# Transfers moved between queues, a finer second fold level, and a new order of issue in a Fourier and two-layer network kernel

## The chip, the core and the metric

One core of a Trainium2 chip runs the whole program. The metric is the device time of one execution in microseconds (us); lower is better. The engines are PE (matrix products; PEld is its weight load), DVE (vector), ACT (scalar), POOL (GpSimd) and SP (which here only issues transfers). Each takes its own instructions strictly in order and waits on semaphores for the others. ACT, SP and POOL can each issue transfers (DMA); all transfers run on the same 16 DMA engines.

## The reference, cut to what matters

```python
X = np.fft.fft(np.fft.fft(x, axis=1), axis=2).real     # x: (4, 3008, 256)
x = X.reshape(12032, 256)
h = x @ moe_w_in;  r = np.maximum(h, 0);  x = (r * r) @ moe_w_out       # 256 -> 2048 -> 256
h = x @ moe2_w_in; g = h * np.cos(h);     y = g @ moe2_w_out
```

The weights arrive as 64-bit floats. The kernel holds each operand of a product as a high and a low part and makes three products (high by high, low by high, high by low).

## The kernel before, in words

**Transform.** The 3008 points of a sequence are folded by symmetry before they are multiplied with cosine and sine tables. `fold_steps(b, t)` folds group `t` (three groups for each of four sequences `b`) on DVE: `mirrored` (1,024 columns), `eo` twice, `half` twice (512 columns each), `quarter` twice (256 columns each), and for two halves of the result `hi` (a copy on ACT that rounds) and `lo` (the rest, on DVE). For the first sequence the steps up to the first `hi`/`lo` pair (0 to 6) come before the first products and the rest (7 to 10) after; products `T` of part 0 (`cos 0`, `sin 0`) need the first pair, those of part 1 the second. `fold_128` folds one separate column (input `x_mid`, tile `zb`). `finish_first` and `finish` turn the products into the transform's columns: an ACT copy `z`, two DVE sums, a rounding copy on ACT (`xh`, `zh`) and the rest on DVE or POOL (`xl`, `zl`).

**Layer one** runs over 12 column blocks and 16 feature groups, in steps of `mm1` (L527, 6 products), `add` (L534 and L223 on DVE, which reads the products out of PSUM), `act` (three ACT passes, L544 to L547), `lo` (four POOL subtractions on quarters, L557) and, three steps later, `mm2` (L569, 12 products). PSUM holds two `h` tiles, so an `mm1` waits until the `add` two products back is done. **Layer two** does the same over 24 half blocks (L621 and L672).

**Weights.** `conv` turns 64-bit words into a high and a low part with an ACT `Abs` (L166), DVE steps and an ACT copy (L179); it runs between the layer-one steps, and `dft` and `split` fold the transform over the feature axis into the first weight matrix.

**Order.** Every piece of work has a name and a time. `at` collects them, `TIMES` overrides the times of several hundred names, and `issue` sorts by time and emits the work. Within one engine the instructions then run in that order. The times are numbers for sorting, about one unit for each layer-one step (4.1 us).

**Queues before.** All transfers go through SP, except these through POOL: the Fourier matrix (`load_cs`), the tables (`load_tab`, and again for each later sequence by `reload_tab`, since the space holds other data in between), the transform's columns read back (`load_z`, L518), the second weights (`load_w2`, L496) and the second layer's input (`load_o`, L609).

Of the kernel before, what the change touches and what calls it, by code (L numbers as in the profile page):

```python
# [10 lines left out]
F32 = mybir.dt.float32  # L11
# [5 lines left out]
AF = mybir.ActivationFunctionType  # L17
# [4 lines left out]
P = 128  # L22
# [8 lines left out]
NT = 3  # L31
# [5 lines left out]
BLK = 512  # L37
# [7 lines left out]
HALVES = [(2 * c + n * w, w) for c, w in BLOCKS for n in range(2)]  # L45
# [12 lines left out]
TW = (2 * J_A, EES + J_EE + 1)  # L58
# [15 lines left out]
class Order:  # L74
# [5 lines left out]
    def at(self, t, fn, name=None):  # L80
        self.ops.append((TIMES.get(name, t), len(self.ops), fn))

# [6 lines left out]
def f32(ap):  # L89
    return ap.bitcast(F32)  # L90
# [3 lines left out]
def kernel(ctx: ExitStack, tc: tile.TileContext, x, x128, cs, tab0, tab1, w_in1, w_out1, w_in2, w_out2, out):  # L94
    nc = tc.nc
    ctx.enter_context(tc.manual_schedule())
    dram = ctx.enter_context(tc.tile_pool(name="dram", bufs=1, space=DRAM))
# [21 lines left out]
    def buf(tag, name, dt=F32, pool=work, bufs=1, shape=(P, 2, BLK)):  # L119
        return pool.tile(list(shape), dt, name=name, tag=tag, bufs=bufs)  # L120
# [35 lines left out]
    def from_f64(st, hi, lo, sh=None):  # L156
# [36 lines left out]
        def lower():  # L193
            r, unit = (w1.bitcast(F32), 2.0 ** -20) if middle is None else (middle, 2.0 ** -36)
            v.scalar_tensor_tensor(out=lo, in0=r, scalar=unit, in1=got["a"].bitcast(F32), op0=ALU.mult, op1=ALU.mult)

        return [size, guard, mask, merge, rest, power] + [join] * (middle is None) + [lower]


    raws, dat, jobs = {}, {}, {}  # L200
    tabs = [[buf(f"t{i}{t}", f"t{i}{t}", F32R, fft, 1, (P, 2, TW[i])) for t in range(NT)] for i in range(2)]
    cs_sb = []
    u128 = [buf(f"u128{p}", f"u128{p}", F32R, fft, 1, (P, 4, NT, B)) for p in "hl"]

    def load_tab(i, t):
        nc.gpsimd.dma_start(out=tabs[i][t], in_=(tab0, tab1)[i][t])

    def reload_tab(i, t):
        tabs[i][t] = buf(f"t{i}{t}", f"t{i}{t}", F32R, fft, 1, (P, 2, TW[i]))
        load_tab(i, t)  # L210

    def load_cs():
        cs_sb.extend(buf(f"cs{p}", f"cs{p}", F32R, fft, 1, (P, 2, D)) for p in "hl")
        for p, src in zip(cs_sb, cs):
            nc.gpsimd.dma_start(out=p, in_=src.rearrange("(k p) d -> p k d", p=P))

    def load_x(b, t, bufs):
        raws[b, t] = bufs
        for i, r in enumerate(bufs):
            nc.sync.dma_start(out=r, in_=x[b, t, i].rearrange("p a e d -> p (a e d)").rearrange("p (h n) -> p h n", h=2))  # L220

    def tt(out, in0, in1, op):
        nc.vector.tensor_tensor(out=out, in0=in0, in1=in1, op=op)  # L223
# [6 lines left out]
    def fold_steps(b, t):  # L230

        x = {}

        def views():
            ra, rb = raws.pop((b, t))
            x["a"], x["b"] = ra, rb
            x["eo"] = units(rb, "p (e a d) -> p e a d", e=2, a=4)

            x["f"] = units(ra, "p (i a b d) -> p i a b d", i=2, a=2, b=2)
            x["fv"] = units(ra, "p (a b d) -> p a b d", a=4, b=2)  # L240

            x["g"] = units(rb, "p (i a d) -> p i a d", i=4, a=2)

            x["src"] = (units(ra, "p (a n) -> p a n", a=4)[:, 1:3], units(rb, "p (a n) -> p a n", a=4)[:, 0:2])

        def mirrored():
            views()
            tt(x["a"], x["a"], x["b"], ALU.add)

        def eo(i):  # L250
            ab = units(x["a"], "p (a e d) -> p a e d", a=4, e=2)
            tt(x["eo"][:, i], ab[:, :, 0], ab[:, :, 1], PM[i])

        def half(i):
            tt(x["f"][:, i], x["eo"][:, :, 0::2], x["eo"][:, :, 1::2], PM[i])

        def quarter(i):
            tt(x["g"][:, i], x["fv"][:, 0:4:3, 0], x["fv"][:, 0:4:3, 1], PM[i])

        def hi(i):  # L260
            if i == 0:
                x["p"] = [buf(f"d{p}", f"d{p}", F32R, fft, NT, (P, 2, 2, 2 * P)) for p in "hl"]
                dat[b, t] = [p.rearrange("p a b (u d) -> p (a b u) d", d=P) for p in x["p"]]
            nc.scalar.activation(x["p"][0][:, i], x["src"][i], AF.Copy)  # L264

        def lo(i):
            tt(x["p"][1][:, i], x["src"][i], f32(x["p"][0])[:, i], ALU.subtract)

        return [mirrored] + [lambda i=i, fn=fn: fn(i) for fn, i in (
            (eo, 0), (eo, 1), (half, 0), (half, 1), (hi, 0), (lo, 0), (quarter, 0), (quarter, 1), (hi, 1), (lo, 1))]  # L270
# [11 lines left out]
    def load_128():  # L282
        raws["mid"] = scratch(2, NT, 4, B)
        nc.sync.dma_start(out=raws["mid"], in_=x128)
# [114 lines left out]
    def load_w1(c, bufs):  # L399
        for k, st in enumerate(bufs):  # L400
            nc.sync.dma_start(out=st.rearrange("p h n -> p (h n)").rearrange("p (n t) -> p n t", t=2),
                              in_=src_in(w_in1, k, c * FCH * P, FCH * P))
            wi[c, k] = st.rearrange("p h n -> p (h n)").rearrange("p (n t) -> p n t", t=2)
# [89 lines left out]
    def load_w2(name, c):  # L493
        parts = w_chunk("a" if name == "in" else "b")
        for p, src in zip(parts, w2_dram[name, c]):
            nc.gpsimd.dma_start(out=p, in_=src)  # L496
        (wi2 if name == "in" else wo2).append(parts)
# [16 lines left out]
    def load_z(k, i):  # L514
        c, w = BLOCKS[k]
        if i == 0:
            load_zb(k, x_buf())
        nc.gpsimd.dma_start(out=xt[1, k][i][:, :, :w], in_=z_dram[i][:, :, c:c + w].rearrange("i p w -> p i w"))  # L518
# [86 lines left out]
    def load_o(k):  # L605
        c, w = HALVES[k]
        parts = x_buf()
        for p, o in zip(parts, o_dram):
            nc.gpsimd.dma_start(out=p[:, :, :w], in_=o[:, :, c:c + w].rearrange("m p w -> p m w"))  # L609
        xt[2, k] = parts  # L610
# [64 lines left out]
    def l2_out(k):  # L675
        c, w = HALVES[k]
        o = buf("AB"[k % 2] + "0", "o")
        a = accs.pop((2, k))
        nc.scalar.activation(o[:, 0, :w], a[:, 0, :w], AF.Copy)
        nc.vector.tensor_copy(o[:, 1, :w], a[:, 1, :w])  # L680
        for m in range(2):
            nc.sync.dma_start(out=out[m][:, c:c + w], in_=o[:, m, :w])
# [42 lines left out]
    def fold(times, b, t):  # L725
        got = []

        def step(j):
            if j == 0:
                got.extend(fold_steps(b, t))  # L730
            got[j]()

        for j, when in enumerate(times):
            at(when, lambda j=j: step(j), ("fold", b, t, j))
# [15 lines left out]
    for t in range(NT):  # L750
        fold([-80 + t + 0.05 * j for j in range(7)] + [0.02 + 0.1 * t + 0.01 * j for j in range(4)], 0, t)
        for i, job in enumerate(JOBS[::2]):
            at(-79.5 + t + 0.01 * i, lambda t=t, i=i, job=job: start_first(job, ps_a, f"acc{i}", (t,)), ("T", 0, i, t))
        at(-79.45 + t, lambda t=t: job_128(0, (t,)), ("job_128", 0, t))
        at(-78.7 + 0.01 * t, lambda t=t: load_tab(1, t), ("tab", 1, t))
# [21 lines left out]
    for key in KEYS:  # L777
        span = 1.5
        if isinstance(key, tuple):
            c, k = key  # L780
            convert(t, span, key, lambda c=c, k=k: conv_w1(c, k))
            if k:
                end = t + span
                at(end, lambda c=c: dft_w1(c), ("dft", c))
                at(end + 0.1, lambda c=c: split_w1(c), ("split", c))
                at(end + 0.8, lambda c=c: load_wc(c), ("load_wc", c))
                if c < NCH - 1:
                    at(end + 0.01, lambda c=c: load_w1(c + 1, pair("B", I32)), ("load_w1", c + 1))
        else:
            convert(t, span, key, lambda f=key: conv_wo1(f))  # L790
            if key < NF - 4:
                at(t + span, lambda f=key + 4: load_wo1(f, buf(f"A{f // 2 % 2}", "wo", I32)), ("load_wo1", key + 4))
        t += span


    for b, (load, start, gap, t1, gap1) in {1: ((14, 21, 21.6), 26, 4, 38.4, 1.5), 2: ((53, 53.5, 54), 54, 4.6, 68, 2), 3: ((76, 76.5, 77), 78, 4.6, 92, 2)}.items():
        for t in range(NT):
            at(load[t], lambda b=b, t=t: load_x(b, t, staged(t)), ("load_x", b, t))
            fold([start + gap * t + gap / 11 * j for j in range(11)], b, t)
        for i in range(2):  # L800
            for t in range(NT):

                at(start + gap * ((i * NT + t) // 2 + 1) + 0.1, lambda i=i, t=t: reload_tab(i, t), ("tab", b, i, t))
        for i, job in enumerate(JOBS):
            def begin(b=b, job=job):
                jobs[b, job] = ps_h.tile([P, 2, BLK], F32, name="h")
                transform(job, jobs[b, job], lhs_of(b), P)

            at(t1 + gap1 * i + 0.2, begin, ("T", b, *job))
            finish(t1 + gap1 * i + 0.9, b, job, lambda b=b, job=job: jobs[b, job], lambda: pair("B", F32R), 0.3)  # L810
# [175 lines left out]
```

## Time and profile before

| what | value |
|---|---|
| median of 3 runs | 1945.47 us (1945.16 to 1946.25) |
| profiled execution | 1946.22 us, of which 1944.4 us lie between its first and last instruction (the span) |
| PE busy | 1893.9 us, 97% of the span |
| ACT, DVE, POOL busy | 76%, 70%, 59% |
| granted PE clock, mean | 0.993 |

Every "idle" below is idle time of an engine before one instruction, with what ended it. A busy share is an average over stages with different limits, so the stages are looked at one by one.

### The profile page before, as it was taken

The numbers are of one execution on the slowest core, as the hardware profiler recorded it, in microseconds if no ns is written. First come the engines' busy times: TensorE is split into PE (matmuls) and PEld (weight loads), VectorE is DVE, ScalarE is ACT, GpSimd is POOL, SyncE is SP. The second block draws the span as 40 slices with busy tenths as digits, with TensorE's granted clock in tenths as the row PEclk, the third lists the DMA queues.
The fourth block names the chain that finished last, engine by engine and source line by source line (L and its number), as shares of the span: only waits on it lengthen the run. The fifth ranks groups of instructions, "written<-read, shape, count | busy, mean of one in ns | idle before, by whom it ended". The sixth has DMA issues, their size and how long they took to land.

```text
span 1944.4 us, 23842 instructions
## 1 busy us (share of the span) xinstructions
PE 1893.9 (97%) x8544; PEld 1572.1 (81%) x8544; DVE 1361.7 (70%) x1563; ACT 1482.8 (76%) x1537; POOL 1139.8 (59%) x1105
## 2 busy tenths in 40 slices
PE   6799999999999999999999999999999999999999
PEld 4577787777888888888888888888888888888887
DVE  7789858769576776765766666666666666666666
ACT  3788777768788888887877777777777777777776
POOL 1567887768787778786544444444444444444442
PEclk8899999999999999999999999999999999999999
DMA  7544443443443343436111111121111111111110
GB/s 274 171 150 136 145 128 140 151 139 113 150 143 132 123 140 117 141 123 192 55 33 32 32 32 33 33 59 37 33 32 33 33 32 44 51 33 33 32 32 21
DMA packets 76153, 173.22 MB, mean 89 GB/s; under 512 B 9072, under 2 KB 32640, under 8 KB 76036
## 3 DMA queue, kind: packets, MB, share of 16 engines
q1 hardware_dynamic: 50692, 108.32, 16.4%
q0 software_dynamic: 25344, 63.39, 11.2%
q8 instruction: 67, 1.10, 0.2%
q14 instruction: 50, 0.41, 0.1%
HBM read 112.90 MB, written 58.79 MB: 88 GB/s over the span
## 4 chain that ended last, share of the span: by engine, by line
PE 77%; DVE 3%; issue 1%; ACT 1%; DVEq 0%; ACTq 0%
PE acc L672 26%; PE h L621 18%; PE acc L569 16%; PE acc L621 9%; PE h L527 8%; PE h L310 1%; DVE s L223 1%; DVE inT L223 1%; DVE u L534 0%; DVE r L635 0%; ACT s L545 0%; ACT s L544 0%; ACT gh L547 0%; ACT dh L264 0%; DVE ol L223 0%
## 5 line engine op out<-in xcount | busy, mean ns | idle before, releaser
L660 POOL TENSOR_TENSOR gl<-r,gh 128x1024 fp32r<-128x1024 f32 (+2 forms) x189 | 445.0, 2355 | 541.5 <-ACT gh L653 471.7
L557 POOL TENSOR_TENSOR gl<-s,gh 128x256 fp32r<-128x256 f32 (+2 forms) x768 | 593.7, 804 | 206.2 <-ACT gh L547 168.7
L635 DVE SCALAR_TENSOR_TENSOR r<-n,h 128x1024 f32<-128x1024 int32 (+2 forms) x129 | 154.7, 1199 | 219.2 <-ACT n L627 199.7
L544 ACT ACTIVATE s<-s 128x1024 f32<-128x1024 f32 (+2 forms) x192 | 199.6, 1040 | 106.6 <-DVE s L223 103.0
L223 DVE TENSOR_TENSOR s<-u,h 128x512 f32<-128x512 f32 (+2 forms) x384 | 242.7, 673 | 23.3 <-POOL gl L557 1.3
L627 ACT ACTIVATE n<-h 128x1024 int32<-128x1024 f32 (+2 forms) x129 | 130.3, 1010 | 160.9 <-PE h L621 160.8
L569 PE MATMUL acc<-gl,wbh 128*128 128x512 f32 (+2 forms) x768 | 237.4, 389 | 4.5 <-POOL gl L557 4.4
L569 PE MATMUL acc<-gh,wbh 128*128 128x512 f32 (+2 forms) x768 | 238.2, 392 | 2.1 <-DVE ol L223 2.1
L635 DVE SCALAR_TENSOR_TENSOR r<-n,r 128x1024 f32<-128x1024 int32 (+2 forms) x192 | 233.4, 1216 | 6.6
L569 PE MATMUL acc<-gh,wbl 128*128 128x512 f32 (+2 forms) x768 | 235.3, 388 | 0.0
L534 DVE SCALAR_TENSOR_TENSOR u<-zb,wc,h 128x512 f32<-128x512 f32 (+2 forms) x192 | 140.6, 732 | 132.5 <-PE h L527 131.5
L643 ACT ACTIVATE r<-r,halfpi 128x1024 f32<-128x1024 f32 (+2 forms) x192 | 218.4, 1137 | 6.2
L545 ACT ACTIVATE s<-s 128x1024 f32<-128x1024 f32 (+2 forms) x192 | 200.5, 1044 | 6.1
L547 ACT ACTIVATE gh<-s 128x1024 fp32r<-128x1024 f32 (+2 forms) x192 | 200.5, 1044 | 6.1
L672 PE MATMUL acc<-gh,wbh 128*128 128x512 f32 (+2 forms) x768 | 202.8, 386 | 0.0
L672 PE MATMUL acc<-gh,wbl 128*128 128x512 f32 (+2 forms) x768 | 202.8, 386 | 0.0
L672 PE MATMUL acc<-gl,wbh 128*128 128x512 f32 (+2 forms) x768 | 202.8, 386 | 0.0
L621 PE MATMUL h<-xh,wah 128*128 128x512 f32 (+2 forms) x516 | 199.0, 386 | 1.1 <-DVE r L223 1.1
L642 ACT ACTIVATE r<-r 128x1024 f32<-128x1024 f32 (+2 forms) x192 | 198.2, 1032 | 1.9 <-DVE r L635 1.8
L621 PE MATMUL h<-xl,wah 128*128 128x512 f32 (+2 forms) x516 | 198.9, 386 | 0.0
L621 PE MATMUL h<-xh,wal 128*128 128x512 f32 (+2 forms) x516 | 198.9, 386 | 0.0
L653 ACT ACTIVATE gh<-r 128x1024 fp32r<-128x1024 f32 (+2 forms) x192 | 197.1, 1027 | 0.4 <-DVE r L223 0.4
(144 smaller groups left out, 3344.1 us busy)
## 6 DMA issues: line engine op xcount, KB each, us to landing
inT<-x_in SPq DMA_DIRECT2D x18, 512.0 KB, 6.6
t<-tab_in POOLq DMA_DIRECT2D x12, 756.0 KB, 5.9
t<-tab_in POOLq DMA_DIRECT2D x12, 752.0 KB, 5.9
oh<-oh SPq DMA_DIRECT2D x16, 512.0 KB, 2.9
ol<-ol SPq DMA_DIRECT2D x16, 512.0 KB, 4.6
xh<-oh POOLq DMA_DIRECT2D x16, 512.0 KB, 4.2
xl<-ol POOLq DMA_DIRECT2D x16, 512.0 KB, 5.1
y_out<-o SPq DMA_DIRECT2D x32, 256.0 KB, 3.7
```

The lines of the kernel that those rows point to most:

```text
L223: nc.vector.tensor_tensor(out=out, in0=in0, in1=in1, op=op)
L544: nc.scalar.activation(s[:, :, :w], s[:, :, :w], AF.Relu)
L545: nc.scalar.activation(s[:, :, :w], s[:, :, :w], AF.Square)
L547: nc.scalar.activation(hi[:, :, :w], s[:, :, :w], AF.Copy)
L557: nc.gpsimd.tensor_tensor(out=lo[:, n, cols], in0=s[:, n, cols], in1=f32(hi)[:, n, cols], op=ALU.subtract)
L569: nc.tensor.matmul(accs[1, k][m][:, n, :w], wt, g[:, n, :w], start=begin and i == 0, stop=end and i == 2)
L621: nc.tensor.matmul(a[:, j, :w], st, mv[:, m, :w], start=m == 0 and q == 0, stop=m == 1 and q == 2)
L635: nc.vector.scalar_tensor_tensor(out=r[:, :, :w], in0=n[:, :, :w], scalar=-c, in1=src[:, :, :w], op0=ALU.mult, op1=ALU.add)
L642: nc.scalar.activation(r[:, :, :w], r[:, :, :w], AF.Abs)
L643: nc.scalar.activation(r[:, :, :w], r[:, :, :w], AF.Sin, bias=halfpi, scale=-1.0)
L660: e.tensor_tensor(out=lo[:, :, :w], in0=r[:, :, :w], in1=f32(hi)[:, :, :w], op=ALU.subtract)
L672: nc.tensor.matmul(accs[2, k][:, m, :w], w_out_t([c[part] for c in wo2], f, m), g[:, j, :w], start=f == 0 and q == 0, stop=f == NF - 1 and ...
```

## The change

1. **Later transfers by SP.** `reload_tab`, `load_z`, `load_w2` and `load_o` (104 issues) go from POOL's queue to SP's. `reload_tab` reads from copies of the six tables in device memory, which six new transfers (`copy_tab`, device memory to device memory, 752 or 756 KB each) make between steps 9 and 15 of layer one.
2. **First transfers by two engines.** Of each pair of transfers of the first weights and of the first sequence, SP issues one and ACT the other; the middle column is loaded by ACT and first. Later pairs stay on SP.
3. **Half of the second fold level later.** For the first sequence `half` (two steps of 512 columns) becomes four steps `some` of 256 columns; two stand ahead of the first `hi`/`lo` pair, two after it, so a group has 13 steps instead of 11.
4. **Output tiles.** `l2_out` uses one tile for each of the two output halves instead of one for both; the very last output half is issued by ACT.
5. **New order.** `TIMES` is replaced (605 names instead of 540).

```diff
+    tab_dram = {(i, t): dram.tile([P, 2, TW[i]], F32, name=f"tab{i}{t}") for i in range(2) for t in range(NT)}
+
+    def copy_tab(i, t):
+        nc.sync.dma_start(out=tab_dram[i, t], in_=(tab0, tab1)[i][t])
     def reload_tab(i, t):
         tabs[i][t] = buf(f"t{i}{t}", f"t{i}{t}", F32R, fft, 1, (P, 2, TW[i]))
-        load_tab(i, t)
+        nc.sync.dma_start(out=f32(tabs[i][t]), in_=tab_dram[i, t])
+    def queues(n):
+        return (nc.sync, nc.sync if n else nc.scalar)
     def load_x(b, t, bufs):
         raws[b, t] = bufs
-        for i, r in enumerate(bufs):
-            nc.sync.dma_start(out=r, ...)
+        for e, i, r in zip(queues(b), range(2), bufs):
+            e.dma_start(out=r, ...)
...
+        def some(ia):
+            i, a = ia
+            tt(x["f"][:, i, a], x["eo"][:, a, 0::2], x["eo"][:, a, 1::2], PM[i])
+        halves = [(some, (0, 1)), (some, (1, 0))] if b == 0 else [(half, 0), (half, 1)]
+        others = [(some, (0, 0)), (some, (1, 1))] if b == 0 else []
-            (eo, 0), (eo, 1), (half, 0), (half, 1), (hi, 0), (lo, 0), (quarter, 0), ...
+            (eo, 0), (eo, 1), *halves, (hi, 0), (lo, 0), *others, (quarter, 0), ...
...
     def load_128():
-        nc.sync.dma_start(out=raws["mid"], in_=x128)
+        nc.scalar.dma_start(out=raws["mid"], in_=x128)
...
     def load_w1(c, bufs):
-        for k, st in enumerate(bufs):
-            nc.sync.dma_start(...)
+        for e, k, st in zip(queues(c), range(2), bufs):
+            e.dma_start(...)
...
     def load_w2(name, c):
-            nc.gpsimd.dma_start(out=p, in_=src)
+            nc.sync.dma_start(out=f32(p), in_=src)
...
     def load_z(k, i):
-        nc.gpsimd.dma_start(out=xt[1, k][i][:, :, :w], ...)
+        nc.sync.dma_start(out=f32(xt[1, k][i])[:, :, :w], ...)
...
     def load_o(k):
-            nc.gpsimd.dma_start(out=p[:, :, :w], ...)
+            nc.sync.dma_start(out=f32(p)[:, :, :w], ...)
...
     def l2_out(k):
-        o = buf("AB"[k % 2] + "0", "o")
-        nc.scalar.activation(o[:, 0, :w], a[:, 0, :w], AF.Copy)
-        nc.vector.tensor_copy(o[:, 1, :w], a[:, 1, :w])
-        for m in range(2):
-            nc.sync.dma_start(out=out[m][:, c:c + w], in_=o[:, m, :w])
+        os = [buf("AB"[k % 2] + str(m), "o", shape=(P, 2, BLK))[:, 0, :w] for m in range(2)]
+        nc.scalar.activation(os[0], a[:, 0, :w], AF.Copy)
+        nc.vector.tensor_copy(os[1], a[:, 1, :w])
+        for m, e in enumerate((nc.sync, nc.scalar if k == len(HALVES) - 1 else nc.sync)):
+            e.dma_start(out=out[m][:, c:c + w], in_=os[m])
...
+    for n, (i, t) in enumerate((i, t) for i in range(2) for t in range(NT)):
+        at(9.37 + n, lambda i=i, t=t: copy_tab(i, t), ("copy_tab", i, t))
```

What the new `TIMES` does to the order, engine by engine. PE: at the start `T sin 0` of group 0 before `T cos 0`; then a dozen single swaps of neighbouring `mm1` and `mm2`, the first of them `mm1` 5 ahead of `mm2` 2. DVE: `fold_128` moves from behind step 2 of the second weight piece to the very front; `split` 0 moves between the two `some` of group 1; the sums of the middle column (`end_128`) move ahead of those of `cos 0`; the late fold steps of the first sequence are reordered so that group 0 comes last; in layer one about 20 `add` move ahead of one or two `conv` steps, and two `fold` steps of later sequences move forward. ACT: the `xh` copies of `cos 0` move ahead of the `z` copy of `sin 0`; the copy of `part` (0, 1) moves from before `split` 1 to after it; a few single swaps. POOL: two swaps near the start.

## Rows read from the trace of the kernel before

**Rows 1.** Busy time by stretch; columns are named in the first line.
```profile
core 0: us, PE busy (x) PEld busy (x) DVE busy (x) ACT busy (x) POOL busy (x), PEclk, DMA share, GB/s
0.00:60.00 60.00, 35.84 (x186) 24.97 (x186) 44.77 (x82) 24.12 (x41) 15.43 (x26) 0.88 0.69 240
60.00:115.00 55.00, 48.19 (x187) 37.08 (x186) 44.45 (x72) 42.45 (x49) 32.13 (x40) 0.91 0.57 180
...
340.00:372.00 32.00, 28.05 (x112) 21.25 (x111) 30.28 (x34) 24.29 (x27) 22.40 (x30) 0.95 0.47 160
...
sum 1944.40, PE 1893.87 PEld 1572.12 DVE 1361.69 ACT 1482.77 POOL 1139.81; mean PE 270.55 PEld 224.59 DVE 194.53 ACT 211.82 POOL 162.83
```

**Rows 2.** Timeline of PE, 344 to 490 us: start, us, instruction, [idle before <-releaser].
```profile
347.94 0.50 PE L527 MATMUL h<-xh,wah 128*128 128x512 f32 x1 [1.24 <-DVE s L223]
...
361.70 0.50 PE L527 MATMUL h<-xh,wah 128*128 128x512 f32 x1 [0.63 <-DVE s L223]
365.25 0.50 PE L527 MATMUL h<-xh,wah 128*128 128x512 f32 x1 [1.88 <-DVE s L223]
...
432.93 0.49 PE L527 MATMUL h<-xh,wah 128*128 128x480 f32 x1 [1.86 <-DVE s L223]
...
486.05 0.95 PE L310 MATMUL h<-t,dh 128*128 128x376 f32 x4 [1.64 <-DVE s L223]
```

**Rows 3.** Busy time in one stretch after the third of these waits; columns as in Rows 1.
```profile
366.30:369.70 3.40, 3.40 (x9) 2.21 (x8) 3.29 (x5) 3.34 (x4) 1.77 (x3) 0.50 0.88 348
```

**Rows 4.** Timeline of DVE, 340 to 482 us.
```profile
340.70 3.39 DVE L223 TENSOR_TENSOR dl<-inT,dh 128x512 fp32r<-128x512 f32 x1 [1.63 <-ACT dh L264]
...
351.59 2.15 DVE L223 TENSOR_TENSOR inT<-inT 128x512 f32<-128x512 f32 x2
...
422.79 8.01 DVE L223 TENSOR_TENSOR inT<-inT 128x512 f32<-128x512 f32 x2
...
481.30 2.74 DVE L223 TENSOR_TENSOR inT<-inT 128x256 f32<-128x256 f32 x1
```

**Rows 5.** Timeline of POOL around the first two DVE rows of Rows 4.
```profile
339.93 0.74 POOL L518 DMA_DIRECT2D xl<-zl  x1
340.69 2.84 POOL L557 TENSOR_TENSOR gl<-s,gh 128x256 fp32r<-128x256 f32 x4
...
351.31 3.73 POOL L557 TENSOR_TENSOR gl<-s,gh 128x256 fp32r<-128x256 f32 x4 [4.18 <-ACT gh L547]
```

**Rows 6.** Timeline of ACT, DVE and PE, 4 to 43 us.
```profile
4.71 0.66 ACT L166 ACTIVATE f64t<-inA 128x512 f32<-128x512 f32 x1 [2.69 <-DMA inA<-w_in]
...
11.02 0.79 DVE L223 TENSOR_TENSOR zb<-zb 128x48 f32<-128x48 f32 x6
...
12.11 0.21 DVE L223 TENSOR_TENSOR u128l<-zb,u128h 128x48 fp32r<-128x48 f32 x1 [0.31 <-ACT u128h L296]
...
16.43 2.62 DVE L223 TENSOR_TENSOR inB<-inB 128x512 f32<-128x512 f32 x4
...
30.66 0.96 PE L310 MATMUL acc<-t,dh 64*128 64x376 f32 x8 [2.12 <-ACT dh L264]
...
37.20 0.41 DVE L223 TENSOR_TENSOR inB<-inB 128x256 f32<-128x256 f32 x1
37.54 0.41 DVE L223 TENSOR_TENSOR in<-in 128x256 f32<-128x256 f32 x1
...
41.44 1.46 DVE L223 TENSOR_TENSOR dl<-in,dh 128x512 fp32r<-128x512 f32 x2
```

**Rows 7.** Transfers: destination<-source, issuing queue, count, size, median us to landing.
```profile
t<-tab_in POOLq DMA_DIRECT2D x12, 752.0 KB, 5.9
...
inA<-w_in SPq DMA_DIRECT2D x2, 512.0 KB, 4.9
```

**Rows 8.** Timeline of ACT at 91 us: the longest wait for a weight transfer.
```profile
91.30 0.69 ACT L166 ACTIVATE mid<-inB 128x512 f32<-128x512 f32 x1 [2.68 <-DMA inB<-w_in]
```

**Rows 9.** Timeline of DVE at the end of the span.
```profile
1940.62 0.66 DVE L680 COPY o<-acc 128x484 f32<-128x484 f32 x1 [4.26 <-ACT o L679]
```

More of the change, by code (lines that the diff above doesn't have):

```diff
@@ L215, in load_cs @@
             nc.gpsimd.dma_start(out=p, in_=src.rearrange("(k p) d -> p k d", p=P))
+    def queues(n):
+        return (nc.sync, nc.sync if n else nc.scalar)
     def load_x(b, t, bufs):
         raws[b, t] = bufs
-        for i, r in enumerate(bufs):
-            nc.sync.dma_start(out=r, in_=x[b, t, i].rearrange("p a e d -> p (a e d)").rearrange("p (h n) -> p h n", h=2))
+        for e, i, r in zip(queues(b), range(2), bufs):
+            e.dma_start(out=r, in_=x[b, t, i].rearrange("p a e d -> p (a e d)").rearrange("p (h n) -> p h n", h=2))
     def tt(out, in0, in1, op):
@@ L267, in lo @@
             tt(x["p"][1][:, i], x["src"][i], f32(x["p"][0])[:, i], ALU.subtract)
+        def some(ia):
[3 more added lines that the diff above has]
+        others = [(some, (0, 0)), (some, (1, 1))] if b == 0 else []
         return [mirrored] + [lambda i=i, fn=fn: fn(i) for fn, i in (
-            (eo, 0), (eo, 1), (half, 0), (half, 1), (hi, 0), (lo, 0), (quarter, 0), (quarter, 1), (hi, 1), (lo, 1))]
+            (eo, 0), (eo, 1), *halves, (hi, 0), (lo, 0), *others, (quarter, 0), (quarter, 1), (hi, 1), (lo, 1))]
     def scratch(*shape):
@@ L399, in load_w1 @@
     def load_w1(c, bufs):
-        for k, st in enumerate(bufs):
-            nc.sync.dma_start(out=st.rearrange("p h n -> p (h n)").rearrange("p (n t) -> p n t", t=2),
+        for e, k, st in zip(queues(c), range(2), bufs):
+            e.dma_start(out=st.rearrange("p h n -> p (h n)").rearrange("p (n t) -> p n t", t=2),
                               in_=src_in(w_in1, k, c * FCH * P, FCH * P))
@@ L517, in load_z @@
             load_zb(k, x_buf())
-        nc.gpsimd.dma_start(out=xt[1, k][i][:, :, :w], in_=z_dram[i][:, :, c:c + w].rearrange("i p w -> p i w"))
+        nc.sync.dma_start(out=f32(xt[1, k][i])[:, :, :w], in_=z_dram[i][:, :, c:c + w].rearrange("i p w -> p i w"))
     def l1_mm1(k, f):
@@ L608, in load_o @@
         for p, o in zip(parts, o_dram):
-            nc.gpsimd.dma_start(out=p[:, :, :w], in_=o[:, :, c:c + w].rearrange("m p w -> p m w"))
+            nc.sync.dma_start(out=f32(p)[:, :, :w], in_=o[:, :, c:c + w].rearrange("m p w -> p m w"))
         xt[2, k] = parts
@@ L750 @@
     for t in range(NT):
-        fold([-80 + t + 0.05 * j for j in range(7)] + [0.02 + 0.1 * t + 0.01 * j for j in range(4)], 0, t)
+        fold([-80 + t + 0.05 * j for j in range(7)] + [0.02 + 0.1 * t + 0.01 * j for j in range(6)], 0, t)
         for i, job in enumerate(JOBS[::2]):
```

2 lines of the change are left out of this document (1 added, 1 removed).

## The prediction

> **What bounds the kernel now.** I read the busy time by stretch first. PE works for 1893.87 of 1944.40 us [rows 1], so 50.5 us of idle time, and the stretches in which PE's clock is granted at its lower level, are all that this change can win; it takes no product away. The idle time is uneven: 24.2 us lie before 60 us, 6.8 us between 60 and 115, and 4.0 us in the 32 us from 340 on, where DVE is busy for 30.28 of 32 [rows 1]. So I asked PE's own timeline there what it waited for. Five waits between 344 and 490 us, 1.24, 0.63, 1.88, 1.86 and 1.64 us, all end with a DVE sum (`add` releasing an `h` tile) [rows 2]: 7.25 us. After the third, PE runs 3.4 us at half its clock (granted 0.50, the 1.2 GHz level) although it is busy all the time [rows 3]; that costs 1.7 us more.
>
> Then: why is DVE late? Its timeline shows four instructions over 2 us between 340 and 482 us; the first took 3.39 us, the longest pair 8.01 us and the last 2.74 us [rows 4]. A 512-column fold step elsewhere takes 2.62 / 4 = 0.655 us [rows 6], and the 256-column step starts 0.34 us after its like (37.20 to 37.54) [rows 6]. So these cost 2.7, 6.7 and 2.3 us too much. They have two inputs in SBUF, and POOL is at work beside them. POOL's timeline shows what is special: the first begins at 340.70, right behind POOL's transfer instruction (339.93 to 340.67), and lasts until POOL's run of four subtractions is nearly over (340.69 to 343.53) [rows 5]. A fold pair that meets such a run without a transfer ahead of it (POOL from 351.31) takes 2.15 us for two: it is delayed by 0.8 us, and POOL's run stretches to 3.73 instead of 2.84 us, so the two take turns [rows 4, 5]. All four long ones follow a POOL transfer instruction by less than 1 us. I read this as: behind a transfer issued by POOL, DVE is not let in until POOL falls idle. Each long one is followed within 8 us by waits of rows 2: 340.70 by 347.94, the second by 361.70 and 365.25, 422.79 by 432.93, 481.30 by 486.05.
>
> **Part 1, later transfers by SP.** POOL no longer issues them, so the long instructions should become ordinary ones (+0.8 us a pair at most). DVE's `add` then comes 2.3 to 6.7 us earlier, more than each wait of PE, so the whole waits go: -7.25 us. The fall of the clock follows only the closest two of them (0.63 and 1.88 within 4 us); without them I expect no fall: -1.7 us. Bounds: 0 if the long instructions come from something else, -9.0 if all goes. I take -8.9, the sum as it stands, since every one of the four has its POOL transfer.
>
> The Trainium skill states a rule against this reading (SBUF — State Buffer, section "SBUF: two separate sides"): DVE and GpSimd share one port pair as an exclusive lock, which whoever starts first holds for one instruction, whoever issued a transfer before. The 0.8 us for a pair agree with it, the 3.39 us do not. By the rule alone the sum would lose the -8.9 us; that is rival A.
>
> SP's queue takes 104 issues more. It is in order: where a `load_z` waits for a `z` store to land, the next `load_x`, table or store waits behind it. These have some steps of 4 us in hand before they are needed; I take 0, with the upper end under rival C. The six table copies move about 4.5 MB through the same engines while weights are loaded; each load behind one lands later by the copy's own time, at most the 5.9 us that a table took [rows 7]. ACT already waits for such loads, up to 2.68 us [rows 8], without PE standing still there. I take +1.0 us, nearer the lower end, since even the longest of ACT's waits now leaves PE at work; bounds 0 and +5.9.
>
> **Parts 2, 3 and the new order at the start.** PE waits 2.12 us at 30.66 for the fold of group 2 [rows 6]. Until then DVE works almost without a break, so its path counts:
> - `fold_128` leaves it: 0.79 + 0.31 (its wait) + 0.21 = -1.30 us [rows 6]. Its new place is idle time of DVE before the first weight conversion, but its last piece waits for an ACT copy queued behind `Abs`, about 0.45 us after `Abs` ends, and the conversion queues behind it: +0.45.
> - `some` instead of `half`: per group 2 x 0.655 become 2 x 0.34, so 3 x 0.63 = -1.89 us.
> - The first weight piece shares the engines with the second instead of preceding it. ACT now waits for it until 4.71 us [rows 6]; the two landed 4.9 us after issue in the mean [rows 7], the first 0.75 to 4.66, so 3.9, the second then 5.9. If both land together, the first comes up to 2.0 us later; if each queue runs at its own speed, 0. I take +0.4, nearer the lower end, since the transfer starts from empty engines. ACT's own five issues and its table load fill time in which it waits anyway (2.69 us idle) [rows 6].
> - `split` 0 between two `some` makes the rounding copy of group 1 wait for one more ACT copy: +0.3.
>
> Sum -2.04 us, just inside PE's 2.12 us of idle time, so the products of group 2 start that much earlier. Next comes `T cos 1`, which needs the late fold steps; they ended at 42.90 (41.44 + 1.46) [rows 6]. They now hold six `some` more, 6 x 0.34 = +2.04, but `end_128` (about 1.1 us) moves into DVE's idle time and two small waits go (1.1 us), so they end near 42.90 - 2.04 + 2.04 - 2.2 = 40.7. `T cos 1` started during them and now must wait for group 0, the last, and needs 1.75 us more: it ends 1.7 us earlier. All that follows to 60 us hangs on it in the same order. I take -1.7 us; bounds -3.0 (the conversion is not late at all, and a clock fall goes too) and +1.0 (the first piece 2 us late).
>
> The remaining swaps (an `add` ahead of a `conv` step, `part` behind `split`) may move waits of about 1 us between 60 and 200 us either way: 0, bounds -4 and +3.
>
> **Part 4, the end.** DVE's last copy waits for ACT's because both write one tile [rows 9]. Side by side, the last transfer is issued about 0.6 us earlier: -0.6 us; 0 if the wait has another cause. Before that PE covers both copies.
>
> **Sum** against the profiled execution of 1946.22 us (1944.4 of span and 1.8 around it): -8.9 + 1.0 - 1.7 - 0.6 = -10.2, so 1936.0 us. The median of the runs stands 0.75 us lower, so 1935.3 us.
>
> **Rivals.**
> - A. *The long DVE instructions are not the transfers' doing*, only an unlucky meeting with POOL's runs. For it: POOL is as busy after the change. Against it: the run from 351.31 met a fold pair and let it in. Then 1945.5 + 1.0 - 1.7 - 0.6 = 1944.2 us: no change.
> - B. *The order and the lighter queues clear other waits too.* DVE is busy 44.45 of 55 us between 60 and 115 [rows 1]; if half of the 6.8 us of idle time there, and a third of the clock's loss (granted 0.91 over 55 us: 0.09 x 55 = 5 us), go as well, 1935.3 - 3.4 - 1.7 = 1930.2 us. Against it: most steps there stay in their old order.
> - C. *SP's queue becomes the wait.* A `load_x` or a weight load stands behind a copy or a waiting `load_z`, DVE reaches the fold or `conv` step first, and being in order it holds up `add` and so PE. Each costs up to 5.9 us [rows 7], with no slack to cover it where ACT already waits, as at 91 us [rows 8]. Four such are 23.6 us: 1935.3 + 23.6 - 1.0 = 1958 us. It decides from three on (17.7 us); against it, the loads keep their lead of several steps.
>
> **How the numbers follow.** Forecast (faster by 4 to 14 us) 0.64, B 0.15, A 0.13, C 0.05, and 0.03 for a start so late that it eats the rest. No change means within 0.2%, 3.9 us, about what a measurement of this kernel tells from none. Of A, 0.01 falls on either side of it, and of the late start 0.02 within it: faster 0.64 + 0.15 + 0.01 = 0.80; same 0.11 + 0.02 = 0.13; slower 0.05 + 0.01 + 0.01 = 0.07. The range must leave out 2 in 10: below, 1928, under B; above, 1943, the forecast's sum with the copies at their upper end (+4.9) and the start at its (+2.7), just short of A. The forecast's own range is 1931 to 1941.5.
>
> **What would show it.** Right: no DVE instruction over 2 us between 100 and 600 us; no POOL transfer after 10 us; PE idle under 1 us in 340 to 372, at full clock; the products of group 2 at about 28.6 us; `T cos 1` ending 1.7 us earlier; DVE's last copy beside ACT's. Wrong: long DVE instructions beside POOL runs that have no transfer ahead (A); PE waits released by `add` behind a DVE or ACT wait on a transfer (C); ACT's first `Abs` after 6 us.

## The result, and the profile after

The changed kernel takes 1929.27 us (median of 4 runs, 1928.63 to 1930.15) against 1945.86 us for the kernel before on the same chip: ratio 0.9914, 95% interval 0.9897 to 0.9931, so 16.6 us less. The forecast was 1935.3 us with a range of 1928 to 1943. The sign and the range were right; the size was not: the time lies below the forecast's own range (1931 to 1941.5) and near rival B's 1930.2. The profiled execution took 1928.63 us, with a span of 1926.9 us.

Busy time by stretch of the changed kernel; columns as in [rows 1].

```profile
0.00:60.00 60.00, 35.12 (x185) 24.19 (x186) 45.62 (x89) 24.93 (x43) 16.40 (x28) 0.91 0.71 241
60.00:115.00 55.00, 50.18 (x200) 38.59 (x199) 46.96 (x75) 44.00 (x49) 28.29 (x38) 0.94 0.64 211
115.00:340.00 225.00, 221.83 (x1017) 182.25 (x1016) 182.51 (x250) 179.65 (x189) 169.92 (x212) 1.00 0.46 158
340.00:372.00 32.00, 30.39 (x141) 24.53 (x141) 25.25 (x35) 25.75 (x28) 23.39 (x30) 1.00 0.46 168
372.00:500.00 128.00, 128.00 (x642) 108.56 (x641) 87.32 (x124) 97.82 (x104) 95.91 (x125) 1.00 0.38 133
```

Against [rows 1], DVE falls from 30.28 to 25.25 us between 340 and 372 and PE rises from 28.05 to 30.39 at full clock. Before 60 us nothing is won: PE 35.12 against 35.84 us. DVE's timeline of the changed kernel, with the steps that answer to [rows 4]: the `dl` behind the wait for `dh`, two pairs of `half`, and a `quarter`.

```profile
333.99 0.82 DVE L232 TENSOR_TENSOR dl<-inT,dh 128x512 fp32r<-128x512 f32 x1 [1.62 <-ACT dh L273]
...
347.93 2.37 DVE L232 TENSOR_TENSOR inT<-inT 128x512 f32<-128x512 f32 x2
...
413.37 2.02 DVE L232 TENSOR_TENSOR inT<-inT 128x512 f32<-128x512 f32 x2
...
466.61 0.60 DVE L232 TENSOR_TENSOR inT<-inT 128x256 f32<-128x256 f32 x1
```

The four took 3.39, 3.87 (a pair, of which the first step is the prediction's second long instruction; its row of the kernel before is shown next), 8.01 (a pair) and 2.74 us before; now 0.82, 2.37, 2.02 and 0.60.

```profile
355.70 3.87 DVE L223 TENSOR_TENSOR inT<-inT 128x512 f32<-128x512 f32 x2
```

PE's timeline of the changed kernel in the same stretch: of the five waits of [rows 2] none is left after 372 us, and `T cos 0` of the last sequence, which waited 1.64 us at 486.05, starts without a wait at 469.57. Two smaller waits stand between 340 and 372 us:

```profile
355.52 0.50 PE L543 MATMUL h<-xh,wah 128*128 128x512 f32 x1 [0.50 <-DVE s L232]
...
358.29 0.73 PE L585 MATMUL acc<-gh,wbh 128*128 128x512 f32 x2 [1.11 <-DVE ol L232]
...
469.57 0.85 PE L326 MATMUL h<-t,dh 128*128 128x376 f32 x4
```

The start is where the forecast fails. ACT's timeline of the changed kernel:

```profile
0.74 0.41 ACTq L300 DMA_DIRECT2D zb<-x_mid  x1
1.18 0.46 ACTq L417 DMA_DIRECT2D inA<-w_in  x1
1.67 0.45 ACTq L229 DMA_DIRECT2D inB<-x_in  x1
2.15 3.69 ACTq L229 DMA_DIRECT2D in<-x_in  x2
5.87 1.28 ACT L166 ACT_TABLE_LOAD   x1 [5.87 <-DMA zb<-x_mid]
7.16 0.66 ACT L166 ACTIVATE f64t<-inA 128x512 f32<-128x512 f32 x1
```

`Abs` starts at 7.16 us and waits for no piece of the weights: before it stand ACT's five issues and the table load. The row of 3.69 us is two issues with a wait between them. The fourth issue ends at 3.18 us and the fifth begins only at 5.50, as a narrower view shows (ACT, then DVE):

```profile
5.50 0.34 ACTq L229 DMA_DIRECT2D in<-x_in  x1
```

```profile
5.50 0.79 DVE L232 TENSOR_TENSOR zb<-zb 128x48 f32<-128x48 f32 x6 [4.63 <-DMA zb<-x_mid]
```

At 5.50 the middle column has landed, ACT's first transfer. In the trace the fifth issue waits for that transfer's semaphore and uses the same one again. In half_unsplit and the three probes, which keep these issues, it begins at 5.74, 5.64, 5.51 and 5.78 us, each time together with DVE's fold of that column. So 2.32 of the 3.69 us are a wait for a landing and not work of issuing. Before, `Abs` started at 4.71 us [rows 6]. The `dh` product of group 2 starts at 30.16 us against 30.66 [rows 6], not at 28.6, and the late fold steps end at 42.37 (41.68 + 0.69) against 42.90, not at 40.7:

```profile
30.16 0.95 PE L326 MATMUL acc<-t,dh 64*128 64x376 f32 x8
...
41.70 1.12 PE L326 MATMUL acc<-t,dh 128*128 128x188 f32 x4 [0.17 <-ACT dh L273]
```

```profile
41.68 0.69 DVE L232 TENSOR_TENSOR dl<-inB,dh 128x512 fp32r<-128x512 f32 x1
```

And at the end DVE's copy still waits for ACT's (ACT's takes 0.57 us from 1922.31), just as in [rows 9], though each now has its own output tile:

```profile
1922.91 0.66 DVE L696 COPY o<-acc 128x484 f32<-128x484 f32 x1 [4.26 <-ACT o L695]
```

### The profile page after: what moved, and what is told of

Its sections match the earlier page's. It is cut to its first block, busy times and chain, and to the rows that moved or that the text cites. A ratio compares the mean times of both kernels' runs of the same rounds, so it can differ in the third digit from the quotient of the medians.

```text
span 1926.9 us, 23833 instructions
## 1 busy us (share of the span) xinstructions
PE 1887.8 (98%) x8544; PEld 1570.3 (81%) x8544; DVE 1346.0 (70%) x1569; ACT 1481.3 (77%) x1537; POOL 1070.1 (56%) x1001
## 4 chain that ended last, share of the span: by engine, by line
PE 81%; DVE 0%; ACT 0%; issue 0%; DVEq 0%; ACTq 0%
PE acc L688 27%; PE h L637 18%; PE acc L585 18%; PE acc L637 9%; PE h L543 9%; PE h L326 1%; DVE s L232 0%; DVE inT L232 0%; DVE u L550 0%; DVE ol L232 0%; ACT s L560 0%; ACT s L561 0%; ACT gh L563 0%; ACT oh L611 0%; DVE o L696 0%
```

## The experiments

To see where each kernel wins, I compare the start of the same product in PE's timelines: kernel less kernel before, in us, negative is earlier. The columns are named products with their start in the kernel before; the last column compares the spans. Each is one profiled execution.

| kernel | `T sin 1`, 44.42 | `mm1` 14, 117.85 | `mm1` 63, 342.45 | `T cos 0` of sequence 3, 486.05 | span |
|---|---|---|---|---|---|
| changed kernel | +0.06 | -2.70 | -5.37 | -16.48 | -17.5 |
| part1_alone | -0.02 | +0.33 | +1.81 | -9.89 | -9.9 |
| part1_copies_late | +0.02 | +0.49 | -0.62 | -12.35 | -12.3 |
| order_alone | -1.92 | -6.71 | -8.42 | -13.74 | -14.8 |
| part1_undone | +1.82 | -0.94 | -3.53 | -8.82 | -9.9 |
| old_order | +3.31 | +4.56 | +5.98 | -5.77 | -5.7 |
| first_by_sp | -0.14 | -3.16 | -5.11 | -16.28 | -17.4 |
| half_unsplit | -0.19 | -3.47 | -4.95 | -16.54 | -17.6 |
| parts_1_4_5 | -2.07 | -6.25 | -7.02 | -18.57 | -19.5 |
| parts_1_4_5_copies_late | -0.81 | -3.06 | -7.12 | -18.64 | -19.7 |

My theory after the result: part 1 wins what the long DVE instructions cost (342 to 486 us), ACT's issues spoil the start, and something else, order or lighter POOL, wins the 5.4 us between 44 and 342. Rivals: A (the transfers are not the cause), and that order and part 1 win the same waits.

**Part 1 by itself.** The kernel before with (cut to the lines that matter):

```diff
-            nc.gpsimd.dma_start(out=p, in_=src)
+            nc.sync.dma_start(out=f32(p), in_=src)
...
-        nc.gpsimd.dma_start(out=xt[1, k][i][:, :, :w], ...)
+        nc.sync.dma_start(out=f32(xt[1, k][i])[:, :, :w], ...)
...
-            nc.gpsimd.dma_start(out=p[:, :, :w], in_=o[...])
+            nc.sync.dma_start(out=f32(p)[:, :, :w], in_=o[...])
...
-        load_tab(i, t)
+        nc.sync.dma_start(out=f32(tabs[i][t]), in_=tab_dram[i, t])
...
+        at(9.37 + n, lambda i=i, t=t: copy_tab(i, t), ("copy_tab", i, t))
```

> The kernel before with part 1 alone: the 104 later transfers by SP and the six table copies; the old order, start and end. Theory (DVE is shut out behind a transfer that POOL issues): no DVE instruction over 2 us between 100 and 600 us, the five PE waits of 1.24, 0.63, 1.88, 1.86 and 1.64 us gone, the time 9 to 12 us below that of before, 1934 to 1937 us. If SP's lighter partner POOL also explains the 5.4 us that the changed kernel gains between 60 and 340 us, up to 17 us below, 1929 us. Rival A (the long instructions are an unlucky meeting with POOL's runs): within 2 us of before, long instructions still there.

Ratio 0.9946 (0.9934 to 0.9959); the span is 9.9 us shorter. All of it is won between 342 and 486 us, 11.7 us; before that it is 1.81 us behind. No DVE instruction with work over 2 us is left between 100 and 600 us. ACT's and then PE's timeline of this kernel show what it lost:

```profile
122.75 0.66 ACT L166 ACTIVATE mid<-wo 128x512 f32<-128x512 f32 x1 [4.98 <-DMA mid<-w_out]
```

```profile
127.40 0.77 PE L532 MATMUL h<-xh,wah 128*128 128x480 f32 x1 [2.54 <-DVE s L228]
```

**The copies' share**, part 1 alone with:

```diff
-        at(9.37 + n, lambda i=i, t=t: copy_tab(i, t), ("copy_tab", i, t))
+        at(20 + 1.5 * n, lambda i=i, t=t: copy_tab(i, t), ("copy_tab", i, t))
```

> Part 1 alone, its six table copies moved from steps 9 to 15 to steps 20 to 28 of layer one, when the weights of layer one are loaded. In part 1 alone ACT waits 4.98 us at 122.75 for a weight transfer and PE 2.71 us behind it at 127.40, and it is 5.97 us behind the kernel before at 128 us. Theory (the copies delay those loads): ACT's wait under 1 us, PE never over 2 us behind the kernel before, 2 to 4 us below part 1 alone, 1930 to 1933 us in the trace. Rival (the weights are late because SP's queue has more to issue in order): the waits stay, within 1 us of part 1 alone.

Ratio 0.9930 (0.9918 to 0.9943), span 2.4 us shorter than with the early copies. ACT's wait for the same transfer:

```profile
118.42 0.68 ACT L166 ACTIVATE mid<-wo 128x512 f32<-128x512 f32 x1 [0.50 <-DMA mid<-w_out]
```

4.98 us has become 0.50, and the kernel is never more than 2 us behind the kernel before (1.94 us, at 86 us). The two intervals overlap; the trace shows where the 2.4 us come from: the copies delayed the weights, and SP's longer queue did not.

**Part 1 undone** in the changed kernel (the edit above backwards).

> The changed kernel with part 1 undone: the later transfers by POOL again, tables read again from the inputs, no copies; new order, start and end kept. Theory: long DVE instructions come back behind POOL's transfers, 9 to 12 us above the changed kernel, 1938 to 1941 us. Rival A: within 2 us of the changed kernel, 1927 to 1931 us. If the new order without part 1 is worth 5 us between 60 and 340 us, that part stays and shows in the trace as a lead over the kernel before at 330 us.

Ratio 0.9932 (0.9919 to 0.9944), span 1934.5 us. Three long DVE instructions are back between 115 and 500 us (3.25, 7.41 and 2.76 us, each behind a POOL transfer). The gap of the ratios to the changed kernel is 0.0018, 3.5 us, less than the 7.6 us between the profiled executions, of which 1.76 us is a later start (the same start program, +1.82 against +0.06); the profiled execution is also the longest of this kernel's five (1936.33 against 1932.9 to 1934.5 us). Both are below the 9 to 12 us expected: without part 1 the new order still wins 5.3 us between 342 and 486 us.

**The order by itself**, the kernel before with the new `TIMES` (both late steps of part 3 empty).

> The kernel before with the new order alone (later transfers by POOL, first by SP, second fold level whole, output tile shared). If the 5.4 us that the changed kernel gains between 60 and 340 us are the order's: 4 to 6 us below before, 1940 to 1942 us, with the lead reached by 330 us. If they are the lighter POOL's (part 1): within 2 us of before at 330 us and at the end. Long DVE instructions beside POOL's transfers in both cases.

Ratio 0.9917 (0.9905 to 0.9929): by the runs as much as the whole change. This was the surprise. DVE's and then PE's timeline of this kernel:

```profile
330.20 1.51 DVE L227 TENSOR_TENSOR dl<-inT,dh 128x512 fp32r<-128x512 f32 x1 [1.62 <-ACT dh L268]
...
344.89 2.12 DVE L227 TENSOR_TENSOR inT<-inT 128x512 f32<-128x512 f32 x2
...
409.03 8.02 DVE L227 TENSOR_TENSOR inT<-inT 128x512 f32<-128x512 f32 x2
...
467.56 2.75 DVE L227 TENSOR_TENSOR inT<-inT 128x256 f32<-128x256 f32 x1
```

```profile
419.18 0.49 PE L538 MATMUL h<-xh,wah 128*128 128x480 f32 x1 [1.87 <-DVE s L227]
...
436.44 0.70 PE L580 MATMUL acc<-gh,wbh 128*128 128x480 f32 x2 [1.66 <-DVE ol L227]
...
472.31 0.96 PE L321 MATMUL h<-t,dh 128*128 128x376 f32 x4 [1.65 <-DVE s L227]
```

Two of the four long steps of the kernel before (at 340.70 and 355.70) are ordinary here although POOL still issues its transfers, because their times have shifted: the `dl` step starts 0.61 us ahead of POOL's transfer (330.81) and not behind it, and the pair starts 0.83 us behind one (it ends at 344.06), after which POOL's own run began only at 344.59. A new long step, 3.26 us at 197.18, has no wait of PE behind it. The other two are as long as before and are followed by the same PE waits (1.87 and 1.65, against 1.86 and 1.64 in [rows 2]), and by one of 1.66 us; its like in the kernel before is not among the prediction's five:

```profile
450.20 0.70 PE L569 MATMUL acc<-gh,wbh 128*128 128x480 f32 x2 [1.65 <-DVE ol L223]
```

So order and part 1 win partly the same waits: alone 14.8 and 9.9 us, together (parts_1_4_5, below) 19.5, which is 5.2 less than their sum, and the order's own gain between 342 and 486 us is 5.3.

The order's other large gain lies between 44 and 118 us. Busy time from 80 to 100 us, first the kernel before, then the order alone, then the changed kernel:

```profile
80.00:100.00 20.00, 16.76 (x60) 12.80 (x59) 13.45 (x22) 14.56 (x17) 9.02 (x12) 0.83 0.63 204
```

```profile
80.00:100.00 20.00, 17.89 (x76) 14.04 (x76) 16.97 (x29) 17.07 (x20) 10.19 (x16) 1.00 0.51 160
```

```profile
80.00:100.00 20.00, 18.39 (x80) 14.41 (x78) 16.26 (x28) 15.71 (x18) 9.90 (x14) 1.00 0.69 230
```

PE's clock is granted in full there, against 0.83: 0.17 x 20 = 3.4 us, and PE is idle 1.1 to 1.6 us less. But part of the clock's gain was lost earlier: the order alone runs at the lower level from 52.90 to 63.14 us, the kernel before only from 55.72 to 62.55. So the whole way from `T sin 1` to `mm1` 14 counts, the same products in both (first the kernel before, then the order alone):

```profile
44.42:117.85 73.43, 60.99 (x266) 46.48 (x265) 58.59 (x94) 55.98 (x68) 42.03 (x54) 0.91 0.55 175
```

```profile
42.51:111.14 68.63, 59.24 (x267) 45.49 (x265) 59.01 (x94) 54.17 (x67) 39.99 (x52) 0.93 0.51 162
```

Of the 4.8 us won, 3.05 are idle time of PE (12.44 us become 9.39) and 1.75 its busy time, the clock's share.

**The order undone** in the changed kernel: the old times, with the late steps of part 3 right ahead of `quarter`.

> The changed kernel with part 5 alone undone: the old times, the two late steps of part 3 right ahead of the quarter steps. Theory (the order and part 1 each remove the waits near 345 to 370 us, and the order alone those of 60 to 115 us): 6 to 9 us above the changed kernel, 1933 to 1936 us. Rival (the order only matters without part 1): within 2 us of the changed kernel.

Ratio 0.9964 (0.9951 to 0.9976), about 10 us above the changed kernel, a little more than the 6 to 9 expected. The gain from 342 to 486 us is whole, 11.75 us; but the start is 3.31 us late, and at 342 us it is 5.98 us behind. Without the new order the rest of the change is worth 5.7 us by the spans, 7.0 by the ratio.

**The start: ACT's issues.** The changed kernel with:

```diff
-        return (nc.sync, nc.sync if n else nc.scalar)
+        return (nc.sync, nc.sync)
...
-        nc.scalar.dma_start(out=raws["mid"], in_=x128)
+        nc.sync.dma_start(out=raws["mid"], in_=x128)
```

> The changed kernel with all first transfers by SP, in the changed order; ACT issues none of them. Theory (ACT's own issues, two of which take 3.69 us together, hold its table load and its first Abs back to 7.16 us): first Abs at 4.7 to 5.2 us, products of group 2 some 2 us earlier (28 us), time 0 to 2.5 us below the changed kernel. Rival (two queues really bring the pieces sooner, and Abs waits for the piece and not for ACT's issues): the second weight piece lands later, Abs is not earlier than 6.5 us or conversion 2 waits as long, time the same or up to 2 us above.

Ratio 0.9895 (0.9880 to 0.9910), span 1927.0 us. ACT's timeline, then PE's:

```profile
0.74 1.28 ACT L166 ACT_TABLE_LOAD   x1 [0.74 <-PEq L989]
5.40 0.66 ACT L166 ACTIVATE f64t<-inA 128x512 f32<-128x512 f32 x1 [3.38 <-DMA inA<-w_in]
```

```profile
28.42 0.95 PE L326 MATMUL acc<-t,dh 64*128 64x376 f32 x8 [0.15 <-ACT dh L273]
```

`Abs` comes 1.76 us sooner and group 2's product at 28.42, so ACT's issues, with the wait among them, were the delay. (5.40 is later than the 4.7 to 5.2 expected: `Abs` now waits for the weights, which land 0.69 us later than before.) But the lead, 3.20 us at the first product of layer one (35.45 us before), is gone at `T sin 1`, 9 us later. Busy time up to 50 us, first here, then in the changed kernel, then with the half level whole too (parts_1_4_5, below):

```profile
30.00:36.00 6.00, 2.65 (x14) 1.14 (x10) 5.10 (x14) 2.10 (x6) 0.00 (x0) 0.90 0.48 129
36.00:42.00 6.00, 5.83 (x18) 4.55 (x18) 5.87 (x14) 3.05 (x6) 1.56 (x2) 0.50 0.83 255
42.00:50.00 8.00, 8.00 (x50) 7.03 (x50) 5.39 (x11) 4.40 (x6) 1.84 (x3) 0.50 0.23 77
```

```profile
36.00:42.00 6.00, 4.87 (x10) 3.07 (x11) 5.87 (x16) 2.56 (x7) 0.00 (x0) 0.50 0.79 231
42.00:50.00 8.00, 8.00 (x78) 6.86 (x77) 6.90 (x13) 5.20 (x8) 3.21 (x5) 0.96 0.43 133
```

```profile
36.00:42.00 6.00, 5.90 (x29) 4.62 (x31) 5.84 (x13) 3.05 (x7) 1.56 (x2) 0.73 0.84 251
42.00:50.00 8.00, 7.79 (x68) 5.87 (x66) 7.08 (x13) 5.14 (x9) 3.78 (x5) 1.00 0.30 109
```

PE is busy without a gap from 42 to 50 us in the first, but at half its clock (0.50, the 1.2 GHz level): 50 products against 78 in the changed kernel. PE had been idle for 3.35 of the six us before 36. So in this execution the start's lead was paid back in clock. It is the longest of this kernel's four, with the lowest mean granted clock: 1928.81 us at 0.993, the others 1926.17 to 1927.31 us at 0.995 to 0.996. The others may have kept some of the lead; no trace of them shows it.

**Part 3 undone**, and **parts 2 and 3 undone** (with the edit above):

```diff
-        halves = [(some, (0, 1)), (some, (1, 0))] if b == 0 else [(half, 0), (half, 1)]
-        others = [(some, (0, 0)), (some, (1, 1))] if b == 0 else []
+        halves = [(half, 0), (half, 1)]
+        others = [(lambda _: None, 0)] * 2 if b == 0 else []
```

> The changed kernel with part 3 alone undone: two whole steps of 512 columns, first transfers still by SP and ACT. Theory (the price is part 3's, since all first transfers by SP changed the end by only 0.1 us): 3 to 5 us below the changed kernel. Rival (the two late weight and table issues of ACT, Abs at 7.16 us, are the price): within 1 us of the changed kernel, because Abs stays at 7.2 us. If the price is shared: 1 to 3 us below.

> The changed kernel without parts 2 and 3: first transfers by SP, second fold level whole for the first sequence; later transfers by SP, output tiles and new order kept. Order alone leads the kernel before by 1.8 us at 60 us and 6.6 at 115 us; with parts 2 and 3 in, that lead was -1.9 and 0.9 us. Theory (part 3 in the new order costs DVE time that the late fold steps need at once): the lead of the order alone comes back beside part 1's, 4 to 5 us below the changed kernel, ratio to before 0.9885 to 0.990, 1922 us in the trace. Rival (what the order gained there and what part 1 gains are the same waits): within 1.5 us of the changed kernel.

Ratios 0.9909 (0.9895 to 0.9922) and 0.9898 (0.9882 to 0.9913), spans 1926.8 and 1924.9 us. With part 3 alone taken out the span is 0.1 us shorter, where 3 to 5 us were expected; the rival, that `Abs` stays late (7.40 us here), fits. With part 2 alone out it is 0.1 us longer; with both out 2.0 us shorter, less than the 4 to 5 us expected. The intervals overlap that of the changed kernel, so the times alone do not settle it. The starts help: five profiled executions with the changed kernel's start (it, part1_undone and the three probes below) have `T sin 1` at +0.06, +1.82, +0.05, +0.31 and +1.88; three with neither part at -1.92, -2.07 and -0.81. So parts 2 and 3 together seem to cost the start about 2.4 us in the mean, but one start program varies by 1.8 us between executions and the groups are small.

**With the copies late too**, parts_1_4_5 with the copies at 20 + 1.5 n.

> The changed kernel without parts 2 and 3 and with the table copies at steps 20 to 28. With the copies in their place that kernel loses 2.6 us of its lead at 130 us and is 1.4 us behind the order alone at 342 us. Theory: 1 to 2.5 us below the kernel without parts 2 and 3, 1922.5 to 1924 us in the trace, and 3 to 4.5 us below the changed kernel. Rival (the waits on weights between 115 and 135 us come from the order, or late copies meet the later sequence's loads): the same or above.

Ratio 0.9892 (0.9875 to 0.9908), 1925.61 us, span 1924.7: the shortest span of all kernels, but not measurably faster than parts_1_4_5. This execution started 1.26 us later and had made that good by 342 us, so the copies may be worth 1.3 us here as well; the runs can't tell.

**Is it the transfer?** Three probes on the changed kernel. First, a transfer of 64 KB that nobody reads, issued by POOL ahead of its four subtractions in 75 steps; second, the same behind them; third, no transfer, but POOL's first quarter subtraction done twice:

```diff
+                if 25 <= i < 100:
+                    d = dram.tile([P, 2, 64], F32, name=f"probe{i}")
+                    nc.gpsimd.dma_start(out=d, in_=tab_dram[0, 0][:, :, :64])
                 l1_lo(k, f)
```

```diff
-            for c in range(0, w, w // 2):
+            for c in range(0, w, w // 2) if n or not twice else (0, 0, w // 2):
```

> The changed kernel with one transfer of 64 KB more in each of the steps 25 to 99 of layer one (75 in all, device memory to device memory, read by nobody), issued by POOL right ahead of its four subtractions. Theory (behind a transfer that POOL issues DVE stays shut out until POOL's run ends): at least 8 DVE instructions over 2 us between 115 and 500 us, where the changed kernel has none, and the time at least 8 us above it. Rival A (the long ones need no transfer, only an unlucky meeting): none or one over 2 us, time within 4 us of the changed kernel.

> The same 75 transfers by POOL, issued right behind its four subtractions, so that POOL mostly falls idle after them until the next rounding copy of ACT. Theory: the lock ends with POOL's idle time, so a third or fewer of the long DVE instructions of the kernel with the transfers ahead, and less than half of its added time. Rival (a transfer by POOL locks DVE out by itself, or the transfers' traffic slows DVE): as many long ones as with the transfers ahead.

> The changed kernel with no transfer more, but POOL does its first quarter subtraction twice in each of the steps 25 to 99 (the same result again), so that its run of 2.84 us becomes some 3.55 us. Theory (it takes the transfer, not POOL's length of work): no DVE instruction with work over 2.5 us between 115 and 500 us; time less than 5 us above the changed kernel. Rival A (long runs of POOL are enough): long ones as with the transfers ahead.

One execution each: 1946.24, 1946.71 and 1944.22 us. DVE instructions with work over 2 us between 115 and 500 us: 12 with the transfers ahead, 11 with them behind, none with the longer run. (The changed kernel has none either.) The same four `half` steps beside POOL, with the transfers ahead, DVE then POOL:

```profile
331.42 6.92 DVE L232 TENSOR_TENSOR inT<-inT 128x512 f32<-128x512 f32 x4
```

```profile
331.39 3.04 POOL L573 TENSOR_TENSOR gl<-s,gh 128x256 fp32r<-128x256 f32 x3
334.38 0.56 POOL L848 DMA_DIRECT2D probe<-tab  x1
334.94 2.84 POOL L573 TENSOR_TENSOR gl<-s,gh 128x256 fp32r<-128x256 f32 x4
337.74 0.56 POOL L848 DMA_DIRECT2D probe<-tab  x1
```

and with the fifth subtraction instead, DVE then POOL:

```profile
333.35 4.29 DVE L232 TENSOR_TENSOR inT<-inT 128x512 f32<-128x512 f32 x4
```

```profile
331.37 9.08 POOL L573 TENSOR_TENSOR gl<-s,gh 128x256 fp32r<-128x256 f32 x10
```

Without a transfer the two engines take turns: POOL's ten subtractions are stretched to 0.91 us each, and DVE's four steps take 1.07 each. Behind a transfer POOL runs its four at their full pace (0.71 each) and DVE's row ends at 338.34, 0.04 us after POOL's next transfer instruction (337.74 + 0.56). So DVE was let in when POOL turned from its run to the next transfer. Rival A is refuted: it takes the transfer. But the transfer is not enough. In the same trace three steps beside such a run (at 312.00, 315.82 and 319.95) took 1.23, 1.23 and 0.96 us, in turns with POOL; there a DVE step of the same kind was at work when POOL's run began. In the kernel before a `dl` step at 209.77 took 0.68 us, though a POOL transfer had ended at 209.08 and POOL's run begun at 209.10. What makes a meeting a long one is open. The rule of the Trainium skill that was weighed in the prediction (SBUF — State Buffer, section "SBUF: two separate sides": a lock held for one instruction) agrees with the probe without transfers. By itself it does not explain the rows behind one, where DVE stood through four instructions of POOL; there the measurement decides.

Two of these expectations failed. The transfers behind the run gave as many long instructions as those ahead: POOL was so full that in all 11 cases its next run began within 0.02 us of the transfer's end, so this probe did not separate "until POOL falls idle" from a lock of another length. And the fifth subtraction, expected to cost under 5 us, made the span 15.6 us longer, nearly as much as the transfers did (17.5 and 18.0 us): 75 steps x 0.7 us of POOL's time have a price of their own (and 1.8 us of it is this execution's start), so the probes tell the mechanism by their count of long instructions and not its price by their time.

## Why the prediction was right, and where it was not

In us, from the table above:

| stretch | forecast | changed kernel |
|---|---|---|
| start, to `T sin 1` | -1.7 | +0.06 |
| to `mm1` 14 | 0 | -2.76 |
| to `mm1` 63 (copies and swaps) | +1.0 | -2.67 |
| to `T cos 0` of sequence 3 (part 1) | -8.9 | -11.11 |
| to the end | -0.6 | -1.0 |
| sum | -10.2 | -17.5 |

**Part 1, -8.9.** The mechanism was right in the main: POOL's transfers make the long instructions, as the probes and the kernels with part 1 show. Size 11.1 to 11.75 us in every kernel that has part 1. The prediction left out a sixth wait, 1.65 us for `ol` at 450.20, which stays where POOL issues the transfers (1.66 us in order_alone and part1_undone) and is gone in the eight kernels in which SP does (the probes aside). (Its "within 8 us" holds from the end of each long step, not from its start: 422.79 to 432.93 is 10.1 us.) "Not let in until POOL falls idle" is too strong as a rule: some steps behind a transfer took turns with POOL. And the 11 us are not what part 1 adds to the new order: of them, 5.3 us would have come from the order anyway.

**The swaps, 0 (bounds -4 and +3).** The step that failed most. The order alone wins 14.8 us: 1.9 at the start, 4.8 to 118 us (3.05 PE's idle time, 1.75 its clock; rival B had 3.4 and 1.7), 1.7 to 342, 5.3 where it avoids two meetings with POOL's transfers, 1.0 after 486. The prediction saw that the long steps were meetings and did not ask what an order that shifts everything by some us does to them. Which swap wins what was not tried; small waits from 118 to 342 us were not traced one by one. That the changed kernel's time lies near rival B's is in part luck: its gain from 44 to 118 us is 2.8 us and not B's 5.1, the start's loss and the larger gains behind 118 us make up the rest.

**The start, -1.7.** Wrong. "ACT's own five issues and its table load fill time in which it waits anyway" was the failing sentence: they end at 7.16 us, not before 4.71, because the fifth issue waits until 5.50 for the landing of the first; so the +0.4 for the first piece became 2.45 us. That `Abs` might start after 6 us the prediction had named as a sign against it. Part 3 does bring group 2's product 1.6 us sooner (30.16 against 31.73 us in half_unsplit, where `Abs` is 0.24 us later), but that lead is gone by 44 us.

**Copies, +1.0.** Bounds right; measured 2.4 us in the old order, with the mechanism foreseen, a weight transfer that lands late; unlike the waits of the kernel before, this one made PE stand still too (2.54 us at 127.40). In the new order the runs can't tell their price from nothing.

**The end, -0.6.** Wrong in cause: with separate output tiles the wait is as it was. Both copies read one `acc` tile; whether that is the reason was not tried. The last 1.0 us are the order's: the order alone, without part 4, wins 1.05 us after 486.

**Signs.** Right: no DVE instruction over 2 us, POOL's last transfer before 10 us, full clock from 340 to 372. Wrong: PE's idle time there is 1.6 us (expected under 1), group 2 at 30.16, `T cos 1`, DVE's last copy. Rival C left no trace beyond the copies.

## What to carry to other kernels

Two edits that end the same wait must not be summed: ask of each what the other leaves. A wait that comes from a meeting of two engines' instructions is also ended by anything that shifts one of them, so a new order is not worth 0 with small bounds when such meetings are in the rows. And issues given to a working engine are instructions of that engine: sum them up to the first instruction that something waits for, and ask of each what it waits for itself.

## What the runs showed of the hardware

- Of five transfers issued by ACT at the start, four took 0.41, 0.46, 0.45 and 1.03 us to issue; the fifth, which uses the first one's semaphore again, was issued only at 5.50 us, when the first had landed. Nine in a row by SP (first_by_sp) took 0.40 to 0.89 us each, and none waited so.
- Behind a transfer that POOL issues, even one of 64 KB between two places in device memory, a DVE instruction with two inputs in SBUF and 512 columns took up to 3.7 us where it takes 1.07 in turns with POOL; but not every one behind such a transfer is long.
- In one execution a lead of 3.20 us at 35 us was gone 9 us later: PE was busy for 13.83 of the 14 us from 36 to 50, but at the lower clock.
- One start program reached the same product up to 1.8 us apart in different executions.
